# An mLSTM and two feed-forward layers: shorter state products, one integer pass, whole-tile stores

## The chip, the core and the metric

The kernel runs on one core of a Trainium2 chip. The time is device microseconds for one execution of the whole program, from inputs in HBM to outputs in HBM. A core has five engines with instruction queues of their own that meet through semaphores: TensorE (PE in the profile, PEld for the loads of its stationary operand), VectorE (DVE), ScalarE (ACT), GpSimd (POOL) and SyncE (SP), which here issues every DMA.

## What is computed

The reference is an mLSTM recurrence for two batches, 8 heads, 768 steps and head dimension 40, followed by two feed-forward layers on 1536 tokens of 320 features, each 320 to 2048 to 320:

```python
for t in range(S):
    m_new = maximum(f_gate[t] + m, i_gate[t])
    f_stab, i_stab = exp(f_gate[t] + m - m_new), exp(i_gate[t] - m_new)
    C = f_stab * C + i_stab * outer(v[t], k[t])
    n = f_stab * n + i_stab * k[t]
    y[t] = sigmoid(o_gate[t]) * (C @ q[t]) / maximum(abs(n @ q[t]), 1)
h = x @ w_in;  x = hinge(h) @ w_out        # hinge: h, 0 or (h + 1)**2 / 4
h = x @ w2_in; x = softplus(h) @ w2_out
```

## The kernel before

**The recurrence** is cut into 12 chunks of 64 steps (c = 0 to 11). The two batches lie in the two halves of the 128 partitions, so a chunk is a token tile of 128 rows. `attention(c, at)` (from line 393) does a chunk: loads of `qk` and `tok`, a scan on VectorE that makes the decay matrix, the products `qkp` (line 450) and `pv` (line 472), the product of the state with the decayed queries (line 480), which adds into `pv`, the new state's product `stp` (line 518), the decay of the state on GpSimd (line 522) and its addition on VectorE (line 528). Each of these products is 8 heads x 2 halves, one small matmul each. A head has 40 rows, but the halves are kept at 64 partitions: the product `stp` takes 64 columns of `tok` as stationary operand, and `state` has 64 rows in each half. A transpose (line 536) then brings the tile's result into the form that the first layer reads. The chunks with `n < EARLY` (4) are those of the first token block.

**The layers** work in three blocks of 512 tokens (j) and 16 slices of 128 hidden features (f): `up` (line 608, 8 matmuls) makes a slice of h, ScalarE and VectorE apply the hinge or softplus and split it into a high and a low part (`split_g`), and `down1` or `down2` (8 or 12 matmuls) adds the slice's part of the result, `LAG` = 3 steps behind `up`.

**The weights** come as 8-byte numbers, 704 of them per partition in one tile, 16 tiles for each layer. `weights(l, f)` (line 553) turns them into 4-byte floats: one load (line 558), two passes of ScalarE (lines 563 and 570: the upper word as a float scaled by 2^-112, and the top mantissa byte of the lower word, scaled to three bits), two integer passes of VectorE (line 574 shifts and joins, line 580 puts the sign in). `weights_split` (line 587) then makes the high part on ScalarE and the low part on VectorE or GpSimd. There are two `raw` buffers, so a load waits for the last pass that reads the tile two before.

**The tables of ScalarE** are loaded by the program where a phase begins (exp, sigmoid, softplus); where an instruction's function is not in the loaded table, the compiler puts one more load in front of it.

**The stores.** After the last slice of a block in `down2` the block's four token tiles are copied from PSUM, in turn by ScalarE and VectorE (lines 758 to 764), and each is stored by two DMAs on SP, one for each batch half (line 769).

**The order** of the instructions on every engine is written out ahead of time by the class `Plan` (line 34). Every task has an engine, a cost in us and a list of what it reads and writes; due times come from the positions (`at`) of TensorE's tasks, and each engine in turn takes the task that is ready and due first. A load's cost comes from `dma(kb)` (line 230), with `after` for its latency. TensorE gets filler matmuls (line 386) where nothing else is ready before the first `up`.

Of the kernel before, what the change touches and what calls it, by code (L numbers as in the profile page):

```python
# [8 lines left out]
F32R = mybir.dt.float32r  # L9
BF16 = mybir.dt.bfloat16  # L10
I32 = mybir.dt.int32
U8 = mybir.dt.uint8
ACTF = mybir.ActivationFunctionType
ALU = mybir.AluOpType
# [4 lines left out]
L = 128  # L19
# [158 lines left out]
def mlstm_moe_moe(ctx: ExitStack, tc: tile.TileContext, gates, qk, tok, ident, w1, w2, out):  # L178
# [36 lines left out]
    def vec(c):  # L215
        return 0.065 + c / 960
# [11 lines left out]
        return 0.1 + c / 430  # L228

    def dma(kb):  # L230
        return dict(cost=max(0.6, kb / 260), after=2.0)

    add = plan.add

# [155 lines left out]
    def attention(c, at):  # L390
# [5 lines left out]
        tk = lambda: tiles[TK]  # L396
        hd = lambda x: x.rearrange("p (h d) -> p h d", h=H)
        half = [slice(64 * i, 64 * i + 64) for i in range(2)]

        def t():  # L400
            nc.sync.dma_start(out=new("qk", QK, [128, 2, H, C]), in_=qk[c])
# [74 lines left out]
        if c > 0:  # L476
            def t():
                for h in range(H):
                    for p in half:
                        nc.tensor.matmul(  # L480
                            tiles["pv", n][p, h, :], tiles[QD][p, h, :], state[p, h, :], start=False, stop=(h == H - 1))
            add("pe", 1.0, t, duty=0.75, reads=[(QD,), (ST,)], writes=[(("pv", n),)], at=at[1] + 0.5)

        def t():
# [27 lines left out]
        if c < NC - 1:  # L512
            def t():
                ps = new("a", ("stp", n), [128, H, V1])
                for h in range(H):
                    k0 = H * V1 + DM + h * D
                    for p in half:
                        nc.tensor.matmul(ps[p, h, :], tk()[p, k0:k0 + 64], tiles[VE][p, h, :], start=True, stop=True)  # L518
            add("pe", 1.1, t, duty=0.75, reads=[(TK,), (VE,)], writes=[(("stp", n),)], new=[("a", ("stp", n))], at=at[1] + 1)
            if c > 0:  # L520
                def t():
                    nc.gpsimd.tensor_tensor(
                        out=state, in0=state, in1=tiles[DK][:, :, C - 1:C].to_broadcast([128, H, V1]), op=ALU.mult)
                add("pool", gps(328), t, port=True, reads=[(DK,)], writes=[(ST,)])

            def t():
                if c > 0:
                    nc.vector.tensor_tensor(out=state, in0=tiles["stp", n], in1=state, op=ALU.add)
                else:
                    nc.scalar.copy(state, tiles["stp", n])  # L530
            add("dve" if c > 0 else "act", vec(328), t, reads=[(("stp", n),)], writes=[(ST,)])

        def t():
            ps = new("a", ("tr", n), [128, 3, L])
# [15 lines left out]
        add("dve", vec(256) + vec(128) + 0.15, t, reads=[(("tr", n),)], writes=[(("xh", j), n), (("xl", j), n)])  # L550


    def weights(l, f):
        R, V, tag = ("raw", l, f), ("v", l, f), ("v", "v2")[l]

        def t():
            r = new("raw", R, [128, WC, 2], I32)
            nc.sync.dma_start(out=r, in_=(w1, w2)[l][f].bitcast(I32).rearrange("p (c w) -> p c w", w=2))
        add("sp", emit=t, writes=[(R,)], new=[("raw", R)], **dma(704))

        def t():
            v = new(tag, V, [128, WC], I32)
            nc.scalar.activation(
                out=v.bitcast(F32), in_=tiles[R][:, :, 1].bitcast(F32), func=ACTF.Copy, scale=2.0 ** -112)
        add("act", act(WC), t, reads=[(R,)] + ([*ATT] if l else []), writes=[(V,)], new=[(tag, V)])

        def t():
            r = tiles[R]
            top = r.rearrange("p c w -> p (c w)").bitcast(U8).rearrange("p (c w) -> p c w", w=8)[:, :, 3]
            nc.scalar.activation(out=r[:, :, 0], in_=top, func=ACTF.Copy, scale=1 / 32, bias=-31 / 64)  # L570
        add("act", act(WC), t, writes=[(R,)])

        def t():
            nc.vector.scalar_tensor_tensor(  # L574
                out=tiles[V], in0=tiles[V], scalar=3, in1=tiles[R][:, :, 0],
                op0=ALU.logical_shift_left, op1=ALU.bitwise_or)
        add("dve", vec(WC), t, port=True, reads=[(R,)], writes=[(V,)])

        def t():
            nc.vector.scalar_tensor_tensor(  # L580
                out=tiles[V], in0=tiles[R][:, :, 1], scalar=-0x80000000, in1=tiles[V],
                op0=ALU.bitwise_and, op1=ALU.bitwise_or)
        add("dve", vec(WC), t, port=True, reads=[(R,)], writes=[(V,)])

        weights_split(l, f, V)
# [146 lines left out]
    def down2(j, f, at):  # L732
# [21 lines left out]
        if e:  # L754
            for i in range(m):
                O = ("o", j, i)

                def t(i=i, O=O):
                    o = new("o", O, [128, DM])
                    if i % 2:  # L760
                        nc.vector.tensor_copy(o, tiles[dk[i]])
                    else:
                        nc.scalar.copy(o, tiles[dk[i]])
                add("dve" if i % 2 else "act", act(DM), t, reads=[*ATT, (dk[i],)], writes=[(O,)], new=[("o", O)])

                def t(i=i, O=O):
                    for b in range(B):
                        r0 = b * S + (t0 // L + i) * C
                        nc.sync.dma_start(out=out[r0:r0 + C, :], in_=tiles[O][64 * b:64 * b + 64, :])
                add("sp", emit=t, reads=[(O,)], **dma(160))  # L770

    softs = {}
    steps = [(l, j, f) for l in range(2) for j in range(len(BLOCKS)) for f in range(NF)]
# [103 lines left out]
```

## Time and profile before

| | |
|---|---|
| median of 3 runs | 442.21 us (441.85 to 443.28) |
| the profiled execution | 442.29 us |
| its span, first to last instruction | 440.5 us |
| mean granted clock of TensorE | 0.996 |
| busy: PE, PEld | 427.5 us (97%), 356.7 us (81%) |
| busy: DVE, ACT, POOL | 318.1 us (72%), 273.4 us (62%), 50.8 us (12%) |
| DMA | 41.11 MB, 12213 packets, 1904 of them under 512 B |

The profile is of one execution. Times in it count from the first instruction. A busy TensorE means that matmuls are in its pipeline. "Idle before" is the time that an engine waited in front of an instruction, with the engine or transfer that released it. In a stretch table "x" counts instructions, and the clock is the granted share of full speed.

### The profile page before, as it was taken

How to read it: one execution, taken by the hardware profiler on the slowest of the kernel's cores; microseconds unless marked ns; L12 is line 12 of the kernel's file. 1: busy time of each engine (PE TensorE's matmuls, PEld its weight loads, DVE VectorE, ACT ScalarE, POOL GpSimd, SP SyncE). 2: the span in 40 equal slices, each digit the busy share in tenths (PEclk: the TensorE clock that was granted, in tenths of full speed). 3: DMA queues.
4: the chain of work that ended last, by engine and by line, in shares of the span. 5: the costliest groups of instructions: out<-in, count | busy, mean ns of one | idle time of the engine just before them, and what ended most of it. 6: DMA issues, size and time to landing. Idle time of an engine off the chain costs nothing.

```text
span 440.5 us, 8190 instructions
## 1 busy us (share of the span) xinstructions
PE 427.5 (97%) x3319; PEld 356.7 (81%) x3319; DVE 318.1 (72%) x494; ACT 273.4 (62%) x473; POOL 50.8 (12%) x62
## 2 busy tenths in 40 slices
PE   8898899999999999999999999999999999999993
PEld 3676688877787878888888888999999999999993
DVE  6889999999968453567888889955565555655551
ACT  5525878767656354468999889655555555555551
POOL 2554112332221121000000000000000000000000
PEclk9999999999999999999999999999999999999998
DMA  5778766447440300014234441000020000110002
GB/s 210 222 255 258 252 208 205 168 149 251 139 179 3 116 1 1 1 49 150 91 119 176 141 132 65 2 0 0 1 58 4 0 1 0 31 31 1 0 1 60
DMA packets 12213, 41.11 MB, mean 93 GB/s; under 512 B 1904, under 2 KB 3568, under 8 KB 12176
## 3 DMA queue, kind: packets, MB, share of 16 engines
q1 hardware_dynamic: 12176, 40.59, 28.2%
q8 instruction: 26, 0.43, 0.4%
q14 instruction: 11, 0.09, 0.1%
HBM read 38.57 MB, written 2.02 MB: 92 GB/s over the span
## 4 chain that ended last, share of the span: by engine, by line
PE 76%; DVE 12%; ACT 6%; DMA 3%; issue 1%; SPq 1%; ACTq 0%
PE h L619 32%; PE d L691 3%; PE d L690 3%; PE d L692 3%; PE d L749 3%; PE a L751 3%; PE a L750 3%; PE a L749 3%; PE d L751 3%; PE d L750 3%; PE qkp L450 2%; DVE v L574 2%; PE pv L472 2%; PE d L686 2%; PE stp L518 2%; PE pv L480 2%
## 5 line engine op out<-in xcount | busy, mean ns | idle before, releaser
L619 PE MATMUL h<-xh,w 128*128 128x512 f32 x576 | 178.3, 392 | 1.9 <-DVE u L636 1.3
L619 PEld LDWEIGHTS h<-xh,w 128*128 128x128 f32 x576 | 108.0, 188 | 25.1 <-DVE u L636 1.8
L672 DVE TENSOR_TENSOR gl<-u,gh 128x512 fp32r<-128x512 f32 x96 | 66.7, 696 | 35.8 <-ACT gh L668 32.2
L668 ACT CAST gh<-u 128x512 fp32r<-128x512 f32 x96 | 59.3, 619 | 48.3 <-DVE u L659 31.4
L619 PE MATMUL h<-xl,w 128*128 128x512 f32 x192 | 75.4, 393 | 1.0 <-DVE xl L546 1.0
L659 DVE TENSOR_TENSOR u<-u,e 128x512 f32<-128x512 f32 x48 | 33.1, 692 | 29.1 <-ACT e L655 29.1
L655 ACT ACTIVATE e<-e 128x512 f32<-128x512 f32 x48 | 30.3, 632 | 32.3 <-DVE e L650 32.3
L636 DVE SCALAR_TENSOR_TENSOR u<-u,h 128x512 f32<-128x512 f32 x48 | 32.7, 682 | 15.5 <-ACT u L632 15.3
L619 PEld LDWEIGHTS h<-xl,w 128*128 128x128 f32 x192 | 36.1, 188 | 6.9 <-DVE xl L546 1.3
L627 ACT ACTIVATE u<-h 128x512 f32<-128x512 f32 x48 | 28.5, 593 | 20.3 <-PE h L619 20.0
L691 PE MATMUL d<-gh,w 128*128 128x512 f32 x96 | 37.5, 391 | 0.0
L690 PE MATMUL d<-gh,w 128*128 128x512 f32 x96 | 37.5, 391 | 0.0
L692 PE MATMUL d<-gl,w 128*128 128x512 f32 x96 | 37.4, 389 | 0.0
L574 DVE SCALAR_TENSOR_TENSOR v<-v,raw 128x704 int32<-128x704 int32 x32 | 29.6, 924 | 9.5 <-ACT raw L570 9.2
L650 DVE SCALAR_TENSOR_TENSOR e<-u,h 128x512 f32<-128x512 f32 x48 | 32.9, 685 | 4.9
L646 ACT ACTIVATE u<-h 128x512 f32<-128x512 f32 x48 | 28.6, 596 | 8.8 <-PE h L619 8.7
L599 DVE TENSOR_TENSOR w<-v,w 128x64 fp32r<-128x64 f32 (+2 forms) x48 | 31.1, 675 | 1.5 <-ACT w L592 1.4
L632 ACT ACTIVATE u<-u 128x512 f32<-128x512 f32 x48 | 30.3, 631 | 0.7
L749 PE MATMUL d<-w,gh 128*128 128x320 f32 x96 | 29.7, 309 | 0.5 <-DVE xl L717 0.5
L751 PE MATMUL a<-w,gl 128*128 128x320 f32 x96 | 29.7, 309 | 0.0
L751 PE MATMUL d<-w,gl 128*128 128x320 f32 x96 | 29.7, 309 | 0.0
L750 PE MATMUL a<-w,gh 128*128 128x320 f32 x96 | 29.6, 309 | 0.0
(92 smaller groups left out, 701.3 us busy)
## 6 DMA issues: line engine op xcount, KB each, us to landing
raw<-in_w_dram SPq DMA_DIRECT2D x32, 704.0 KB, 4.1
qk<-in_qk_dram SPq DMA_DIRECT2D x12, 512.0 KB, 4.8
tok<-in_tok_dram SPq DMA_DIRECT2D x12, 496.0 KB, 4.3
dec<-scr_d SPq DMA_DIRECT2D x22, 128.0 KB, 4.0
out_dram<-o SPq DMA_DIRECT2D x24, 80.0 KB, 2.1
consts<-in_ident_dram SPq DMA_DIRECT2D x1, 132.0 KB, 2.2
gf<-in_gates_dram SPq DMA_DIRECT2D x1, 48.0 KB, 1.9
gi<-in_gates_dram SPq DMA_DIRECT2D x1, 48.0 KB, 1.9
```

Source lines behind the costliest of these rows:

```text
L574: nc.vector.scalar_tensor_tensor(out=tiles[V], in0=tiles[V], scalar=3, in1=tiles[R][:, :, 0], op0=ALU.logical_shift_left, op1=ALU.bitwise_or)
L619: nc.tensor.matmul(hp, a, x, start=(i == 0), stop=(i == len(ops) - 1))
L650: nc.vector.scalar_tensor_tensor(out=new("e", E, [128, n]), in0=tiles[M], scalar=-2.0, in1=tiles[HP], op0=ALU.mult, op1=ALU.add)
L659: nc.vector.tensor_tensor(out=tiles[M], in0=tiles[M], in1=tiles[E], op=ALU.add)
L668: nc.scalar.copy(new("gh", GH, [128, n], F32R), tiles[G])
L672: nc.vector.tensor_tensor(out=new("gl", GL, [128, n], F32R), in0=tiles[G], in1=tiles[GH].bitcast(F32), op=ALU.subtract)
L690: nc.tensor.matmul(d[i], hi[:, k], gh, start=s, stop=False)
L691: nc.tensor.matmul(d[i], lo[:, k], gh, start=False, stop=False)
L692: nc.tensor.matmul(d[i], hi[:, k], gl, start=False, stop=e)
L749: nc.tensor.matmul(d, gh[:, k], hi, start=s, stop=False)
L750: nc.tensor.matmul(d, gh[:, k], lo, start=False, stop=False)
L751: nc.tensor.matmul(d, gl[:, k], hi, start=False, stop=e)
```

## The change

It touches five places. The state product reads 40 of the 64 rows of each half, in all chunks after the first, and for chunks from 4 on `stp` takes 40 columns as stationary operand, writes 40 rows in each half, and the state is added in two instructions of 40 partitions; the planner gives that product 0.75 us instead of 1.1. The weights' load writes its bytes one place further in the tile. ScalarE's two passes become two Prelu instructions: the first turns the top byte, read as a signed integer, into a value in V, the second turns V, in place, into the integer of sign and upper exponent bits; VectorE then shifts the word that begins at the fourth byte by five and joins it, in one pass. A token tile is stored by one DMA from 128 partitions, with a target of three dimensions (batch, row, feature), and the last tile is copied in two halves by ScalarE and VectorE. The planner reckons loads with 330 GB/s and at least 0.45 us, instead of 260 GB/s and 0.6.

```diff
--- before.py
+++ after.py
@@ -9,6 +9,7 @@
 F32R = mybir.dt.float32r
 BF16 = mybir.dt.bfloat16
 I32 = mybir.dt.int32
+I8 = mybir.dt.int8
 U8 = mybir.dt.uint8
 ACTF = mybir.ActivationFunctionType
 ALU = mybir.AluOpType
@@ -228,7 +229,7 @@
         return 0.1 + c / 430
 
     def dma(kb):
-        return dict(cost=max(0.6, kb / 260), after=2.0)
+        return dict(cost=max(0.45, kb / 330), after=2.0)
 
     add = plan.add
 
@@ -396,6 +397,7 @@
         tk = lambda: tiles[TK]
         hd = lambda x: x.rearrange("p (h d) -> p h d", h=H)
         half = [slice(64 * i, 64 * i + 64) for i in range(2)]
+        keys = [slice(64 * i, 64 * i + D) for i in range(2)]
 
         def t():
             nc.sync.dma_start(out=new("qk", QK, [128, 2, H, C]), in_=qk[c])
@@ -476,9 +478,9 @@
         if c > 0:
             def t():
                 for h in range(H):
-                    for p in half:
+                    for p, k in zip(half, keys):
                         nc.tensor.matmul(
-                            tiles["pv", n][p, h, :], tiles[QD][p, h, :], state[p, h, :], start=False, stop=(h == H - 1))
+                            tiles["pv", n][p, h, :], tiles[QD][k, h, :], state[k, h, :], start=False, stop=(h == H - 1))
             add("pe", 1.0, t, duty=0.75, reads=[(QD,), (ST,)], writes=[(("pv", n),)], at=at[1] + 0.5)
 
         def t():
@@ -514,9 +516,10 @@
                 ps = new("a", ("stp", n), [128, H, V1])
                 for h in range(H):
                     k0 = H * V1 + DM + h * D
-                    for p in half:
-                        nc.tensor.matmul(ps[p, h, :], tk()[p, k0:k0 + 64], tiles[VE][p, h, :], start=True, stop=True)
-            add("pe", 1.1, t, duty=0.75, reads=[(TK,), (VE,)], writes=[(("stp", n),)], new=[("a", ("stp", n))], at=at[1] + 1)
+                    for p, k in zip(half, keys):
+                        o, w = (p, 64) if n < EARLY else (k, D)
+                        nc.tensor.matmul(ps[o, h, :], tk()[p, k0:k0 + w], tiles[VE][p, h, :], start=True, stop=True)
+            add("pe", 1.1 if n < EARLY else 0.75, t, duty=0.75, reads=[(TK,), (VE,)], writes=[(("stp", n),)], new=[("a", ("stp", n))], at=at[1] + 1)
             if c > 0:
                 def t():
                     nc.gpsimd.tensor_tensor(
@@ -524,11 +527,12 @@
                 add("pool", gps(328), t, port=True, reads=[(DK,)], writes=[(ST,)])
 
             def t():
-                if c > 0:
-                    nc.vector.tensor_tensor(out=state, in0=tiles["stp", n], in1=state, op=ALU.add)
+                if c == 0:
+                    nc.scalar.copy(state, tiles["stp", n])
                 else:
-                    nc.scalar.copy(state, tiles["stp", n])
-            add("dve" if c > 0 else "act", vec(328), t, reads=[(("stp", n),)], writes=[(ST,)])
+                    for r in [slice(0, 128)] if n < EARLY else keys:
+                        nc.vector.tensor_tensor(out=state[r], in0=tiles["stp", n][r], in1=state[r], op=ALU.add)
+            add("dve" if c > 0 else "act", vec(328) * (1 if n < EARLY else 2), t, reads=[(("stp", n),)], writes=[(ST,)])
 
         def t():
             ps = new("a", ("tr", n), [128, 3, L])
@@ -550,36 +554,33 @@
         add("dve", vec(256) + vec(128) + 0.15, t, reads=[(("tr", n),)], writes=[(("xh", j), n), (("xl", j), n)])
     def weights(l, f):
         R, V, tag = ("raw", l, f), ("v", l, f), ("v", "v2")[l]
 
         def t():
-            r = new("raw", R, [128, WC, 2], I32)
-            nc.sync.dma_start(out=r, in_=(w1, w2)[l][f].bitcast(I32).rearrange("p (c w) -> p c w", w=2))
+            r = new("raw", R, [128, 2 * WC + 2], I32)
+            nc.sync.dma_start(out=r.bitcast(U8)[:, 1:8 * WC + 1], in_=(w1, w2)[l][f].bitcast(U8))
         add("sp", emit=t, writes=[(R,)], new=[("raw", R)], **dma(704))
 
         def t():
             v = new(tag, V, [128, WC], I32)
+            top = tiles[R].bitcast(I8).rearrange("p (c w) -> p c w", w=8)[:, 1:WC + 1, 0]
+            nc.scalar.activation(out=v.bitcast(F32), in_=top, func=ACTF.Prelu, bias=-56.0, alpha=2.0 ** -40)
+        add("act", act(WC), t, reads=[(R,)] + ([*ATT] if l else []), writes=[(V,)], new=[(tag, V)])
+
+        def t():
             nc.scalar.activation(
-                out=v.bitcast(F32), in_=tiles[R][:, :, 1].bitcast(F32), func=ACTF.Copy, scale=2.0 ** -112)
-        add("act", act(WC), t, reads=[(R,)] + ([*ATT] if l else []), writes=[(V,)], new=[(tag, V)])
-
-        def t():
-            r = tiles[R]
-            top = r.rearrange("p c w -> p (c w)").bitcast(U8).rearrange("p (c w) -> p c w", w=8)[:, :, 3]
-            nc.scalar.activation(out=r[:, :, 0], in_=top, func=ACTF.Copy, scale=1 / 32, bias=-31 / 64)
-        add("act", act(WC), t, writes=[(R,)])
-
-        def t():
+                out=tiles[V], in_=tiles[V].bitcast(F32), func=ACTF.Prelu, scale=2.0 ** 27, bias=112 * 2.0 ** -13,
+                alpha=2.0 ** 40)
+        add("act", act(WC), t, writes=[(V,)])
+
+        def t():
+            mid = tiles[R].rearrange("p (c w) -> p c w", w=2)[:, 0:WC, 1]
             nc.vector.scalar_tensor_tensor(
-                out=tiles[V], in0=tiles[V], scalar=3, in1=tiles[R][:, :, 0],
-                op0=ALU.logical_shift_left, op1=ALU.bitwise_or)
-        add("dve", vec(WC), t, port=True, reads=[(R,)], writes=[(V,)])
-
-        def t():
-            nc.vector.scalar_tensor_tensor(
-                out=tiles[V], in0=tiles[R][:, :, 1], scalar=-0x80000000, in1=tiles[V],
-                op0=ALU.bitwise_and, op1=ALU.bitwise_or)
+                out=tiles[V], in0=mid, scalar=5, in1=tiles[V], op0=ALU.logical_shift_right, op1=ALU.bitwise_or)
         add("dve", vec(WC), t, port=True, reads=[(R,)], writes=[(V,)])
 
         weights_split(l, f, V)
@@ -755,19 +756,27 @@
             for i in range(m):
                 O = ("o", j, i)
 
+                def copies(parts, j=j, i=i, O=O):
+                    for e, c0, c1 in parts:
+                        def t(e=e, c0=c0, c1=c1):
+                            o = tiles[O] if O in tiles else new("o", O, [128, DM])
+                            o, d = o[:, c0:c1], tiles[dk[i]][:, c0:c1]
+                            if e == "dve":
+                                nc.vector.tensor_copy(o, d)
+                            else:
+                                nc.scalar.copy(o, d)
+                        add(e, act(c1 - c0), t, reads=[*ATT, (dk[i],)], writes=[(O, c0)],
+                            new=[("o", O)] if c0 == 0 else [])
+
+                if j == len(BLOCKS) - 1 and i == m - 1:
+                    copies([("act", 0, DM // 2), ("dve", DM // 2, DM)])
+                else:
+                    copies([("dve" if i % 2 else "act", 0, DM)])
+
                 def t(i=i, O=O):
-                    o = new("o", O, [128, DM])
-                    if i % 2:
-                        nc.vector.tensor_copy(o, tiles[dk[i]])
-                    else:
-                        nc.scalar.copy(o, tiles[dk[i]])
-                add("dve" if i % 2 else "act", act(DM), t, reads=[*ATT, (dk[i],)], writes=[(O,)], new=[("o", O)])
-
-                def t(i=i, O=O):
-                    for b in range(B):
-                        r0 = b * S + (t0 // L + i) * C
-                        nc.sync.dma_start(out=out[r0:r0 + C, :], in_=tiles[O][64 * b:64 * b + 64, :])
-                add("sp", emit=t, reads=[(O,)], **dma(160))
+                    r0 = (t0 // L + i) * C
+                    nc.sync.dma_start(out=out.rearrange("(b s) d -> b s d", b=B)[:, r0:r0 + C, :], in_=tiles[O])
+                add("sp", emit=t, reads=[(O, 0), (O, DM // 2)], **dma(160))
 
     softs = {}
     steps = [(l, j, f) for l in range(2) for j in range(len(BLOCKS)) for f in range(NF)]
```

## Rows read from the trace of the kernel before

**Rows 1.** Busy time by stretch: PE, PEld, DVE, ACT, POOL, clock, DMA share, GB/s.
```profile
10.00:41.40 31.40, 30.04 (x549) 21.18 (x547) 27.87 (x46) 13.52 (x32) 15.76 (x20) 1.00 0.74 240
41.40:60.00 18.60, 16.08 (x176) 12.29 (x177) 18.47 (x29) 15.56 (x27) 4.77 (x7) 1.00 0.78 240
60.00:121.00 61.00, 60.57 (x617) 48.65 (x616) 58.08 (x98) 44.50 (x78) 16.77 (x16) 1.00 0.56 185
...
260.00:278.00 18.00, 17.52 (x90) 15.08 (x89) 16.39 (x25) 16.80 (x29) 0.00 (x0) 1.00 0.24 81
```

**Rows 2.** Timeline of PE at the first `up`: start, us, instruction.
```profile
41.38 0.51 PE L619 MATMUL h<-xh,w 128*128 128x512 f32 x1
```

**Rows 3.** Timeline of the last 8 us.
```profile
432.92 4.94 SPq L769 DMA_DIRECT2D out_dram<-o  x8
...
433.79 0.49 DVE L761 COPY o<-a 128x320 f32<-128x320 f32 x1 [0.39 <-PE a L751]
```

**Rows 4.** Chain of waits: start, us, what.
```profile
38.41 6.59 DMA tok<-in_tok_dram
...
140.92 1.08 PE qkp L450 x32
...
147.87 0.93 PE stp L518 x32
...
281.14 1.84 PE h L619 x8
284.74 1.84 PE h L619 x8
```

**Rows 5.** Groups by form: busy us, mean ns | idle before, releaser.
```profile
L632 ACT ACTIVATE u<-u 128x512 f32<-128x512 f32 x48 | 30.3, 631 | 0.7
...
L580 DVE SCALAR_TENSOR_TENSOR v<-raw,v 128x704 int32<-128x704 int32 x32 | 29.4, 918 | 0.1
...
L570 ACT ACTIVATE raw<-raw 128x704 int32<-128x704 uint8 x32 | 27.0, 844 | 0.0
L592 ACT CAST w<-v 128x704 fp32r<-128x704 f32 x32 | 24.8, 777 | 6.6 <-DVE v L580 5.8 <-PE d L692 0.4
...
L528 DVE TENSOR_TENSOR state<-stp,state 128x328 f32<-128x328 f32 x10 | 4.7, 466 | 0.1
```

**Rows 6.** Stretch before the first `up`, L574 alone: us, DVE busy (x instructions).
```profile
10.00:41.40 31.40, 1.76 (x2) 1.00 0.74 240
```

**Rows 7.** DMA issues on the page: KB each, median us to landing.
```profile
raw<-in_w_dram SPq DMA_DIRECT2D x32, 704.0 KB, 4.1
...
tok<-in_tok_dram SPq DMA_DIRECT2D x12, 496.0 KB, 4.3
...
out_dram<-o SPq DMA_DIRECT2D x24, 80.0 KB, 2.1
```

**Rows 8.** Waits of SP's queue: us in total, times, longest.
```profile
SPq L558 <- DVE v L580: 154.0, 27, 44.8
```

**Rows 9.** Timeline of ACT: table loads and weight passes.
```profile
154.54 1.28 ACT L799 ACT_TABLE_LOAD   x1
...
168.35 1.28 ACT L489 ACT_TABLE_LOAD   x1
...
258.97 1.28 ACT L655 ACT_TABLE_LOAD   x1 [1.34 <-DVE e L650]
...
262.67 0.85 ACT L563 ACTIVATE v<-raw 128x704 f32<-128x704 f32 x1
...
273.96 0.87 ACT L570 ACTIVATE raw<-raw 128x704 int32<-128x704 uint8 x1
```

**Rows 10.** DMA of the last 8.5 us: packets, MB, share.
```profile
DMA packets 640, 0.66 MB, mean 77 GB/s; under 512 B 128, under 2 KB 640, under 8 KB 640
...
q1 hardware_dynamic: 640, 0.66, 31.7%
```

**Rows 11.** Busy time by stretch, 12 to 14 us.
```profile
12.00:14.00 2.00, 2.00 (x11) 0.98 (x12) 1.91 (x4) 1.93 (x8) 2.00 (x3) 1.00 1.02 364
```

More of the change, by code (lines that the diff above doesn't have):

```diff
@@ L562, in t @@
             v = new(tag, V, [128, WC], I32)
-            nc.scalar.activation(
-                out=v.bitcast(F32), in_=tiles[R][:, :, 1].bitcast(F32), func=ACTF.Copy, scale=2.0 ** -112)
+            top = tiles[R].bitcast(I8).rearrange("p (c w) -> p c w", w=8)[:, 1:WC + 1, 0]
+            nc.scalar.activation(out=v.bitcast(F32), in_=top, func=ACTF.Prelu, bias=-56.0, alpha=2.0 ** -40)
         add("act", act(WC), t, reads=[(R,)] + ([*ATT] if l else []), writes=[(V,)], new=[(tag, V)])
         def t():
-            r = tiles[R]
-            top = r.rearrange("p c w -> p (c w)").bitcast(U8).rearrange("p (c w) -> p c w", w=8)[:, :, 3]
-            nc.scalar.activation(out=r[:, :, 0], in_=top, func=ACTF.Copy, scale=1 / 32, bias=-31 / 64)
-        add("act", act(WC), t, writes=[(R,)])
+            nc.scalar.activation(
+                out=tiles[V], in_=tiles[V].bitcast(F32), func=ACTF.Prelu, scale=2.0 ** 27, bias=112 * 2.0 ** -13,
+                alpha=2.0 ** 40)
+        add("act", act(WC), t, writes=[(V,)])
         def t():
+            mid = tiles[R].rearrange("p (c w) -> p c w", w=2)[:, 0:WC, 1]
             nc.vector.scalar_tensor_tensor(
-                out=tiles[V], in0=tiles[V], scalar=3, in1=tiles[R][:, :, 0],
-                op0=ALU.logical_shift_left, op1=ALU.bitwise_or)
-        add("dve", vec(WC), t, port=True, reads=[(R,)], writes=[(V,)])
-        def t():
-            nc.vector.scalar_tensor_tensor(
-                out=tiles[V], in0=tiles[R][:, :, 1], scalar=-0x80000000, in1=tiles[V],
-                op0=ALU.bitwise_and, op1=ALU.bitwise_or)
+                out=tiles[V], in0=mid, scalar=5, in1=tiles[V], op0=ALU.logical_shift_right, op1=ALU.bitwise_or)
         add("dve", vec(WC), t, port=True, reads=[(R,)], writes=[(V,)])
```

## The prediction

> **What bounds the kernel now.** I read the page's busy times first (TensorE leads), then a table of stretches, the chain of waits, the costliest groups by form, and last the two ends. The stretches show where TensorE isn't busy. In 60 to 121 us it has 0.43 us of idle time and in 260 to 278, the busiest later stretch of ScalarE and VectorE, 0.48, all at granted clock 1.00, the 2.4 GHz level [rows 1]. So behind 60 us only shorter TensorE work moves the end. Ahead of it VectorE is the full engine: 18.47 of 18.6 us in 41.4 to 60, where TensorE idles 2.5 us, and 27.87 of 31.4 us in 10 to 41.4, where the first `up` starts [rows 1, 2]. The end is a tail: the last copy starts at 433.79, and eight stores that SP issues one after another from 432.92 fill the time to 440.5 [rows 3]. The profiled execution took 442.29, 1.8 us more than its span and 0.1 over the median of 442.21; I sum against 442.29.
>
> **Part 1, 40 stationary columns (c = 4 to 10, seven `stp` tasks).** All seven stand behind 60 us, on the bound. The chain of waits gives one `stp` 0.93 us for 32 records, and `qkp`, with the same 64 stationary columns but 64 moving ones instead of 41, 1.08 [rows 4]. No row has 40 stationary columns. At least nothing is saved; in proportion to the columns it is 0.93 x 24/64 = 0.35 us. The nearest rows say that 23 columns on the other operand are worth 0.15 us. I take 0.2: 7 x 0.2 = **-1.4 us** (0 to -2.4). The state product over 40 instead of 64 rows keeps its moving and stationary columns: 0. VectorE's add becomes two of 40 partitions; it has as many elements per partition, so 7 x 0.47 = 3.3 us are added [rows 5]. They are hidden by what part 2 takes from VectorE; without that they would land in stretches with 3 us free in 61.
>
> **Part 2, one integer pass.** It removes one of two passes of 0.92 us for each of 32 weight tiles, 29.4 us of VectorE [rows 5]. ScalarE keeps two: the byte pass stays like L570 (844 ns, the same stride), the second reads 704 contiguous words as the cast of L592 does (777), so ScalarE gets 32 x 0.07 = 2.1 us back, hidden. The second now reads what the first wrote; the hinge has such an in-place pair on the same engine, and it idled 0.7 us in 48 [rows 5]: 0. What is the VectorE time worth? Two tiles' passes stand before 41.4 us [rows 6]. There the gain is at most two passes, 1.8 us; from there to 60 at most the idle 2.5 us: 4.3 together. What is late next there is TensorE's own order and the loads. Behind 60 us it buys at most the 0.9 us of idle time.
>
> The load lands one byte off. No row has such a target. At best it costs nothing, at worst the moving part of the 4.1 us (all above the 2.1 of a small store [rows 7]) doubles, 2 us a tile. I take 0, as the loads' issue mostly waited for VectorE: 154 us in 27 waits of SP for L580, the last pass of a tile [rows 8].
>
> **Part 3, loads at 330 GB/s in the planner.** This changes no work, only order, on SP and behind it on every engine. A `tok` load issued at 38.41, behind two weight loads, took 6.59 us instead of 4.3 [rows 4, 7]. If the new order puts weight loads ahead of two more such loads on the chain, 2 x 2.3 = 4.6 us are lost. With part 2's gain the early stretch is worth between +4.6 and -4.3; I take **-2**, since every weight load also waits for one pass less.
>
> **Part 4, ScalarE's tables.** The trace shows three loads in order: the table for softplus loaded at 154.54, `Abs` made a load of 1.28 us necessary at 168.35, and Softplus another at 258.97 [rows 9]. So the softplus table does not hold every function, and the new Prelu may be one that it lacks. After the first Softplus ScalarE still has weight passes, in five groups between Softplus instructions, the first at 262.67 and the last at 273.96 [rows 9]. If Prelu is missing, each costs a load there and one back: 10 x 1.28 = 12.8 us on an engine that is busy 16.80 of 18 us there [rows 1]. If not, nothing. ScalarE's idle time (1.2) and about one step of 3.6 us [rows 4] absorb some of it, since `down2` runs three steps behind `up` and two `h` buffers stand between: 12.8 - 1.2 - 3.6 = 8. With a pass less the weight tiles come through sooner, so I count two groups, 5.1 us, and of these nearly all absorbed: **+1** (0 to +11.6).
> The Trainium skill, "ScalarE: Activation LUTs", section "Table sets: the hidden batching unit", says that the cheap functions (relu, copy, identity, abs) are filler in every set. The load for `Abs` at 168.35 says otherwise; by the page's sentence this term would rather be 0.
>
> **Part 5, one store for a token tile.** Before, 8 stores of 64 rows left 640 packets in the last 8.5 us: 512 of 1280 bytes and 128 under 512 bytes, 16 for each store, one for each engine [rows 10]. The new store has on the DRAM side an outermost extent of 2 (the batch halves), then 64 rows. No row has a transfer whose outermost extent is under 16, so both ends are open.
> Spread over 16 engines: four issues instead of eight. At 4.94 / 8 = 0.62 us each [rows 3] from 432.92 the last starts at 434.8, after the halved copy; landing takes 2.1 us [rows 7] and four more packets per engine 0.34: it ends at 437.2, **-3.3 us**.
> Dealt by the outermost extent: two engines carry four stores, 256 packets each. A store's packet costs 31.7% x 16 x 8.5 us / 512 = 84 ns when 16 engines write at once; the fastest loads, 364 GB/s at share 1.02, come to 22.3 GB/s for an engine or 57 ns for 1280 bytes [rows 10, 11]. Two engines alone are nearer to the second; I take 60 ns: 15.4 us, and 2.1 - 0.34 = 1.76 for issue and completion, 17.2 us from the first issue where there were 7.6: **+9.6** (8.9 to 15.7). The earlier blocks' stores have some 58 us each and nothing behind them: hidden.
> I take the second as the likelier, since rows of 64 and 16 have always been dealt whole to 16 engines and a deal by the outermost dimension is the plainest that does this, while nothing shows one that looks further in.
> The Trainium skill, "DMA: Bandwidth & Descriptors", section "Rules for kernel authors", states it so: an outermost dimension of c < 16 confines the whole transfer to at most c engines. The trace agrees only as far as its 16 small packets per store go. By its section on two partition halves (one transfer of 128 partitions is better than two) part 5 would instead gain, as in the first reading.
>
> **Sum.** 442.29 - 1.4 - 2 + 1 + 9.6 = **449.5 us**.
>
> **The rivals.**
> Spread stores (the other side: faster): the tail gives 3.3 us back instead. For it: all stores so far ran on 16 engines, and SP's eight issues of 0.62 do set the tail. Against: the outer extent of 2. It decides between four and eight engines: 128 packets x 60 ns and 1.76 are 9.4 us, over today's 7.6, 64 packets are 5.6. 442.29 - 1.4 - 2 + 1 - 3.3 = 436.6.
> Tables or late loads eat it: the stores are spread, but Prelu switches tables in all five groups (+8 instead of +1: 443.6) or the loads go the wrong way (+4.6 instead of -2: 443.2). For it: the `Abs` load, the 6.59 us. Against: weights that finish before 259 need no switch.
> The change doesn't do what it says: 40 columns run no faster; 1.4 us more in either case (450.9 or 438.0).
>
> **How the numbers follow.** Two engines 0.62; spread 0.30; spread with the gain eaten 0.08, about 443.4. The two-engine case alone lies in 446 to 457 (its tail from +8.9 to +15.7, the early stretch and the tables each way). For eight in ten the range must reach into the spread case: 435 to 455. A difference under 0.3% (1.3 us) can't be told from none here. Faster: 0.30 and a quarter of 0.08, 0.32. Same: 0.04, from the third case and the lucky end of the first. Slower: 0.64.
>
> **What would show it.** Part 1: `stp` from c = 4 on at 0.7 to 0.75 us instead of 0.93. Part 2: 32 integer passes and VectorE some 26 us less busy; the first `up` before 41.4. Part 4: table loads beyond five, behind 259. Part 5: 2 small packets for a store instead of 16 and a tail of about 17 us after the first of the last four issues; 16 small packets and an end 3 us after the last copy would prove me wrong, and the time would be near 436. A first `up` after 42 would say that the order of loads cost more than the pass gave.

## The result, and the profile after

The changed kernel takes 449.13 us (median of 4 runs, 448.74 to 450.19) where the kernel before takes 442.08 in the same comparison: a ratio of 1.015 (95% interval 1.0127 to 1.0174), slower by 7 us. The forecast was 449.5. Medians and ratios here and below leave out executions that were disturbed as a whole; of two experiments the profiled execution was such a one, and no trace of them is used.

The profiled execution took 448.74 us, with a span of 447.0. The page: busy time by engine, granted clock in 40 slices (the last two, 8 and 5, hold the tail, in which TensorE has nothing more to do), packets.
```profile
PE 426.2 (95%) x3315; PEld 353.6 (79%) x3315; DVE 292.7 (65%) x467; ACT 273.0 (61%) x474; POOL 52.7 (12%) x64
...
PEclk9999999999999999999999999999999999999985
...
DMA packets 11853, 41.11 MB, mean 92 GB/s; under 512 B 1544, under 2 KB 3208, under 8 KB 11816
```
VectorE is 25.4 us less busy (318.1 before). The packets under 512 bytes fell by 360: 12 stores with 2 each in place of 24 with 16.

Busy time by stretch, columns as in [rows 1]:
```profile
10.00:41.40 31.40, 30.80 (x558) 21.40 (x554) 26.43 (x49) 16.50 (x36) 16.96 (x19) 1.00 0.88 288
41.40:60.00 18.60, 17.39 (x183) 13.23 (x184) 17.04 (x30) 16.06 (x29) 6.58 (x7) 1.00 0.60 196
60.00:121.00 61.00, 61.00 (x598) 49.29 (x597) 50.43 (x87) 44.05 (x78) 15.74 (x19) 1.00 0.57 192
```
Behind 60 us TensorE no longer waits, and VectorE has 7.7 us less to do in 60 to 121. But the first `up` comes at 42.25 us, 0.87 later than in [rows 2], and it waits for ScalarE's copy of the transposed tokens. One trace doesn't fix this number: in six traces whose kernels have the same instructions on TensorE in the same order (this one and five of the variants below) the first `up` comes at 41.1 to 42.7 us. The timeline of PE:
```profile
42.25 0.49 PE L620 MATMUL h<-xh,w 128*128 128x512 f32 x1 [1.17 <-ACT xh L545]
```
From the first `up` to the start of the last matmul (less 0.04 us), first before, then after: length, busy time of PE and PEld, and so on.
```profile
41.38:433.40 392.02, 388.59 (x2718) 331.81 (x2719) 283.10 (x435) 254.43 (x430) 31.88 (x35) 1.00 0.24 78
```
```profile
42.25:430.80 388.55, 388.19 (x2718) 329.20 (x2719) 258.40 (x405) 249.93 (x424) 31.86 (x37) 1.00 0.22 74
```
The middle is shorter by 3.47 us, and nearly all of it is idle time: 3.43 before, 0.36 after. TensorE's busy time fell by only 0.40, though the state products became shorter. Groups of instructions by form, and one `stp` in the chain of waits:
```profile
L521 PE MATMUL stp<-ve,tok 64*40 64x41 f32 x224 | 5.5, 198 | 0.0
...
L582 DVE SCALAR_TENSOR_TENSOR v<-raw,v 128x704 int32<-128x704 int32 x32 | 28.4, 891 | 10.4 <-ACT v L575 10.4
```
```profile
65.38 0.61 PE stp L521 x32
```
0.61 us instead of the 0.93 of [rows 4], seven times, is 2.3 us. As much is lost again in the `up` products, which run at 394 to 395 ns. The group of line 619 before, and of line 620 after:
```profile
L619 PE MATMUL h<-xh,w 128*128 128x512 f32 x576 | 178.3, 392 | 1.9 <-DVE u L636 1.3 <-DVE w L599 0.4
L619 PE MATMUL h<-xl,w 128*128 128x512 f32 x192 | 75.4, 393 | 1.0 <-DVE xl L546 1.0
```
```profile
L620 PE MATMUL h<-xh,w 128*128 128x512 f32 x576 | 180.5, 395 | 1.2 <-ACT xh L545 1.2
L620 PE MATMUL h<-xl,w 128*128 128x512 f32 x192 | 75.7, 394 | 0.0
```
That is 2.5 us more in the same 768 products; the other 0.6 us by which TensorE's busy time fell are not assigned. Last the tail, which answers to [rows 3]. The last matmul before, then the timeline after, and the DMA of 430.2 to 447 us after:
```profile
433.44 0.31 PE L751 MATMUL a<-w,gl 128*128 128x320 f32 x1
```
```profile
430.32 6.09 SPq L778 DMA_DIRECT2D out_dram<-o  x4
...
430.84 0.31 PE L752 MATMUL a<-w,gl 128*128 128x320 f32 x1
```
```profile
GB/s 0 0 0 24 40 34 30 18 37 49 49 49 49 49 49 55 49 49 49 49 49 49 49 49 52 52 49 49 49 49 49 49 49 49 55 49 43 0 0 0
DMA packets 520, 0.66 MB, mean 39 GB/s; under 512 B 8, under 2 KB 520, under 8 KB 520
...
q1 hardware_dynamic: 520, 0.66, 11.2%
```
From the start of the last matmul to the end it takes 447.0 - 430.84 = 16.2 us, where it took 440.5 - 433.44 = 7.1. Four stores leave 8 small packets, 2 each, and the same 0.66 MB flows at 49 GB/s, where [rows 10] had a mean of 77 with idle time in it. SP's four issues take longer than the eight before (6.09 us against 4.94), but they end at 430.32 + 6.09 = 436.4, and the data flow on at 49 GB/s for another 9 us. So the rate sets this tail, not the issuing. In sum: +0.87 (first `up`) - 3.07 (idle time) - 0.40 (TensorE's work) + 9.10 (tail) = +6.5 us, the difference of the two spans.

### The profile page after: what moved, and what is told of

Read it like the earlier page. It is cut to its first block, busy times and chain, and to the rows that moved or that the text cites. A ratio compares the mean times of both kernels' runs of the same rounds, so it can differ in the third digit from the quotient of the medians.

```text
span 447.0 us, 8134 instructions
## 1 busy us (share of the span) xinstructions
PE 426.2 (95%) x3315; PEld 353.6 (79%) x3315; DVE 292.7 (65%) x467; ACT 273.0 (61%) x474; POOL 52.7 (12%) x64
## 4 chain that ended last, share of the span: by engine, by line
PE 87%; DMA 4%; DVE 3%; ACT 1%; issue 1%; SPq 0%; POOL 0%; ACTq 0%; DVEq 0%
PE h L620 38%; PE d L692 5%; PE d L691 5%; PE d L693 5%; PE d L751 3%; PE a L751 3%; PE a L752 3%; PE d L752 3%; PE d L750 3%; PE a L750 3%; PE d L687 3%; PE d L688 2%; PE qkp L452 2%; PE pv L474 2%; DMA raw<-in_w_dram 2%; PE pv L482 1%
## 5 line engine op out<-in xcount | busy, mean ns | idle before, releaser
L620 PE MATMUL h<-xh,w 128*128 128x512 f32 x576 | 180.5, 395 | 1.2 <-ACT xh L545 1.2
L620 PEld LDWEIGHTS h<-xh,w 128*128 128x128 f32 x576 | 108.0, 188 | 25.4 <-ACT xh L545 1.4
L673 DVE TENSOR_TENSOR gl<-u,gh 128x512 fp32r<-128x512 f32 x96 | 67.7, 706 | 41.1 <-ACT gh L669 37.0
L582 DVE SCALAR_TENSOR_TENSOR v<-raw,v 128x704 int32<-128x704 int32 x32 | 28.4, 891 | 10.4 <-ACT v L575 10.4
L571 ACT ACTIVATE v<-raw 128x704 f32<-128x704 int8 x32 | 27.0, 844 | 8.1 <-DMA raw<-in_w_dram 4.8
L600 DVE TENSOR_TENSOR w<-v,w 128x704 fp32r<-128x704 f32 (+2 forms) x46 | 29.4, 666 | 3.7 <-ACT w L593 3.5
```

Of the source, the lines that this page charges most:

```text
L620: nc.tensor.matmul(hp, a, x, start=(i == 0), stop=(i == len(ops) - 1))
L673: nc.vector.tensor_tensor(out=new("gl", GL, [128, n], F32R), in0=tiles[G], in1=tiles[GH].bitcast(F32), op=ALU.subtract)
```

## The experiments

My theory: the stores cost 9 us and hide a gain of some 2 us, made of the shorter state products and the emptied early stretch, less a slower pace of the `up` products. Rivals for each stand with the expectations. "Two stores" is the changed kernel with the stores of before, the base for most of what follows.

### Part 5, the stores

**Two stores.** The changed kernel with
```diff
-nc.sync.dma_start(out=out.rearrange("(b s) d -> b s d", b=B)[:, r0:r0 + C, :], in_=tiles[O])
+for b in range(B):
+    r0 = b * S + (t0 // L + i) * C
+    nc.sync.dma_start(out=out[r0:r0 + C, :], in_=tiles[O][64 * b:64 * b + 64, :])
```


> The changed kernel with the stores of before: two DMAs of 64 rows for each token tile, everything else and the order of every engine as in the changed kernel. Theory (the one store is dealt to two engines): the last matmul starts where it does in the changed kernel (430.8 us), the last four tiles leave 128 small packets instead of 8, and the end comes 7 us after the last matmul as before instead of 16: span 437.9, about 439.7 us. Rival (the tail is long because SP's issue of a store became longer, or because the halved last copy comes later): the tail stays over 12 us and the time over 445.

Measured 440.09 us, 0.9948 of before (0.9919 to 0.9978). The tail is back at 437.3 - 430.34 = 7.0 us, and it has 128 small packets again. Timeline of the last matmul, and the DMA of 429 to 437.4 us:
```profile
430.34 0.31 PE L752 MATMUL a<-w,gl 128*128 128x320 f32 x1
```
```profile
DMA packets 640, 0.66 MB, mean 78 GB/s; under 512 B 128, under 2 KB 640, under 8 KB 640
```

**The kernel before with one store**: the same edit the other way round in the kernel before, nothing else.

> The kernel before with nothing changed but the store: one DMA of 128 partitions for each token tile. Theory: 8 small packets in the tail, about 50 GB/s over it, 16.7 us from the first of the last four issues to the end instead of 7.6: 442.1 + 9.1 = 451.2 us. Rival (one store is as good as two and the loss came from another part): 439 to 442.

Measured 451.06 us, 1.0197 (1.018 to 1.0215): +8.8. The two together show part 5 as cause, with and without the other parts: 449.13 - 440.09 = 9.0 there, 8.8 here. Its DMA from 432 to 449 us is the changed kernel's, 520 packets with 8 under 512 bytes.

**Two stores in the last block alone**, the single store kept in the first two blocks.
```diff
+if j < len(BLOCKS) - 1:
     nc.sync.dma_start(out=out.rearrange("(b s) d -> b s d", b=B)[:, r0:r0 + C, :], in_=tiles[O])
+else:
+    for b in range(B):
+        nc.sync.dma_start(out=out[b * S + r0:b * S + r0 + C, :], in_=tiles[O][64 * b:64 * b + 64, :])
```


> The changed kernel with one store for a tile in the first two token blocks and two stores in the last. Theory (the earlier blocks' slow stores have 58 us each and nothing behind them): the same as with two stores everywhere, 439.7 us, within 0.3%. Rival (a transfer that runs 14 us on two engines holds up something, a buffer of the copies or the fetching of instructions): slower than that by more than 0.3%.

Measured 441.55 us, 0.9977 (0.995 to 1.0004). The median is 1.5 us, or 0.33%, above that of two stores, just past the mark of the rival, but the intervals overlap, and no cost of the earlier blocks' stores is shown. The profiled execution has the short tail (442.3 - 435.32 = 7.0 us). It is 5 us longer than the one of two stores ahead of that, but not where the stores are: the first is issued at 325.9 us, and from 300 to 420 us both kernels get through the same 667 matmul records. The time is lost in the early stretch, where TensorE's granted clock fell to the 1.2 GHz level for a while. The stretch table of this kernel (PE, PEld, DVE, ACT, POOL, clock, DMA share, GB/s):
```profile
40.00:42.00 2.00, 1.16 (x5) 0.54 (x5) 2.00 (x4) 1.08 (x3) 1.53 (x1) 1.00 1.04 319
42.00:44.00 2.00, 1.63 (x5) 1.23 (x5) 1.69 (x5) 0.54 (x1) 1.44 (x2) 0.73 0.72 218
44.00:46.00 2.00, 2.00 (x6) 1.54 (x6) 1.40 (x2) 1.50 (x3) 0.00 (x0) 0.50 0.26 46
```
The fall stands behind 1.21 us of idle time in 40 to 44 us. The executions scatter with it: of ten of two stores, the six with a mean clock of 0.995 or 0.996 lie at 438.6 to 440.1 us, the two with 0.988 at 442.7 and 444.3. What decides whether the clock falls is open: the changed kernel's trace has 1.21 us of idle time in the same 4 us and kept 1.00.

**Two queues.** Two stores, those of the second batch in the last block issued by ScalarE.
```diff
-nc.sync.dma_start(out=out[r0:r0 + C, :], in_=tiles[O][64 * b:64 * b + 64, :])
+q = nc.scalar if b and j == len(BLOCKS) - 1 else nc.sync
+q.dma_start(out=out[r0:r0 + C, :], in_=tiles[O][64 * b:64 * b + 64, :])
```


> The changed kernel with two stores for a tile, and in the last block the second batch half issued by ScalarE's queue instead of SP's. Theory (what is left of the tail is SP issuing eight stores of 0.62 us one after another): the last store is issued some 2.3 us earlier, span 435.6, 437.4 us. Rival (the landing of the data sets the end, or ScalarE's copies are held up by its own issues): no better than with one queue, 439.7.

Measured 437.74 us, 0.9882 (0.9842 to 0.9922), as expected; of its four executions two took 436.0 and 436.3 us and two 439.2. The timeline of its last 6 us:
```profile
431.83 2.66 SPq L780 DMA_DIRECT2D out_dram<-o  x4
432.32 0.59 ACTq L780 DMA_DIRECT2D out_dram<-o  x1
...
432.35 0.31 PE L752 MATMUL a<-w,gl 128*128 128x320 f32 x1
...
433.06 1.78 ACTq L780 DMA_DIRECT2D out_dram<-o  x3
```
Eight issues take 3.0 us side by side instead of 4.94 in a row, and the tail is 437.4 - 432.35 = 5.1 us where it was 7.0. So before the change it was the issuing, not the engines' rate, that set the tail; the change halved the issues and lost the engines.

### Parts 1 to 3, the middle

**Part 1 undone** (on two stores): 64 columns and one addition again, with their costs in the planner; the state is still read over 40 rows.
```diff
-o, w = (p, 64) if n < EARLY else (k, D)
+o, w = p, 64
```


> The changed kernel with the two 64-row stores of before, and with part 1 undone: all state products of the seven later blocks take 64 stationary columns again, at their old cost in the planner. Compared with the kernel that has only the two stores given back (440.09 us). Theory: a block's chain of 32 state products costs 0.93 us of TensorE with 64 columns and 0.61 us with 40, so seven blocks give 7 x 0.32 = 2.3 us back: 442.4 us, with the product's mean near 228 ns where it was 198, and TensorE busy all the same. Rival: the 32 records only overlap differently and the engine is not held longer: 440.1 us, and the steps of the state stage are as long as with 40 columns.

Measured 441.39 us, 0.9977 (0.9948 to 1.0005): 1.3 us more than two stores, between the two numbers, and the intervals overlap. Not decided by itself.

**Part 1 alone**, in the kernel before, with its planner costs.

> The kernel before with part 1 alone: 40 stationary columns for the state products of the seven later blocks, contraction over 40 rows where the state is read, and the two additions of 40 partitions instead of one of 128. Weight passes, planner costs, addresses and stores are those of before. Theory: 32 records take 0.61 us instead of 0.93, 7 x 0.32 = 2.3 us less TensorE time on the path that sets the end: 440.0 us, with VectorE about 7 x 0.48 = 3.4 us busier and no new wait. Rival: the gain is eaten by VectorE, which sets the pace of the early stretch and now has a second addition of 0.48 us in each of the later blocks: 441.5 to 442.5 us, with idle time of TensorE ahead of up products grown by as much as the products save.

Measured 441.77 us, 0.9992 (0.9974 to 1.0011). The 2.3 us (a ratio of 0.9948) lie outside; the rival's number was right. The products did become shorter:
```profile
L520 PE MATMUL stp<-ve,tok 64*40 64x41 f32 x224 | 5.6, 200 | 0.0
```
but the profiled execution lost the gain in the early stretch, where its clock fell twice (stretches of 4 us, columns as above):
```profile
18.00:22.00 4.00, 4.00 (x78) 3.71 (x75) 1.46 (x4) 1.35 (x4) 0.72 (x1) 0.61 0.29 90
46.00:50.00 4.00, 4.00 (x29) 3.02 (x28) 4.00 (x7) 2.27 (x4) 1.03 (x1) 0.70 0.50 162
```
The rival's mechanism, more idle time ahead of `up` products, is not shown by that: 2.1 us before `up` here and 2.7 in the kernel before. What is shown is that part 1 alone moves the time by less than it takes from TensorE. Part of that is the clock: the five executions with a mean clock of 0.995 or more have a median of 441.28 us, the fourteen such of the kernel before 442.03, which is 0.75 us. Where the rest of the 2.3 goes stays open.

**Part 2 undone** (on two stores): the four passes and the raw tile of before.
```diff
-nc.scalar.activation(out=v.bitcast(F32), in_=top, func=ACTF.Prelu, bias=-56.0, alpha=2.0 ** -40)
+nc.scalar.activation(out=v.bitcast(F32), in_=tiles[R][:, :, 1].bitcast(F32), func=ACTF.Copy, scale=2.0 ** -112)
...
+nc.vector.scalar_tensor_tensor(
+    out=tiles[V], in0=tiles[V], scalar=3, in1=tiles[R][:, :, 0],
+    op0=ALU.logical_shift_left, op1=ALU.bitwise_or)
...
```


> The changed kernel with the two 64-row stores of before and with part 2 undone: the weights are unpacked by the passes of before (VectorE builds the low word in a pass of its own), and the raw tile has its old size, so the weight tiles stand at the addresses of before. Two things are expected by the theory that part 2 emptied the early stretch and that the weight tile's address sets the pace of the up products: VectorE is busy some 25 us longer and TensorE waits again between 41.4 and 60 us, about 2 us more than the 0.45 us of the kernel with two stores, while the mean of the up products goes from 394 back to 389 ns (-2.5 us): 439 to 441 us, and the two parts can be read apart in the trace. Rival 1: the early stretch was emptied by part 3 (the order) alone: no wait comes back and the time is 437.6 us. Rival 2: the up products' pace has nothing to do with the address: they stay at 394 ns, and the time is 442 to 443 us.

Measured 448.82 us, 1.0104 (1.0056 to 1.0152): 8.7 us more than two stores by the medians, 6.9 by the ratios, and above all three expectations. The first `up` comes at 45.15, and TensorE waits for VectorE and ScalarE ahead of it and behind: in 60 to 121 us, where the kernel with two stores has no idle time, it idles 5.45 us. Timeline, stretch and longest waits of PE (us in total, times, longest):
```profile
45.15 0.51 PE L626 MATMUL h<-xh,w 128*128 128x512 f32 x1
```
```profile
60.00:121.00 61.00, 55.55 (x537) 42.80 (x537) 58.18 (x93) 43.17 (x75) 14.20 (x14) 1.00 0.59 190
```
```profile
PE qkp L452 <- DVE y L505: 2.0, 1, 2.0
PE tr L540 <- ACT y L511: 1.9, 1, 1.9
```
One part of the expectation held: the `up` products are back at 392 and 393 ns. The kernel with part 1 alone has the same passes and the same products, but the order of the old planner costs (and the last copy in one piece), and takes 441.77 us. So most of the loss comes with the order that the planner makes of the old passes with the costs of parts 1 and 3, and what part 2 is worth depends on it. Which of those costs does it (part 3's is the likelier) was not separated.

**Part 3 undone** (on two stores).
```diff
-return dict(cost=max(0.45, kb / 330), after=2.0)
+return dict(cost=max(0.6, kb / 260), after=2.0)
```


> The changed kernel with the two 64-row stores of before, and with part 3 undone: the order is made with 260 GB/s and a floor of 0.6 us for a load, as before. Theory: the early stretch was emptied by the fewer VectorE passes, and part 3 only moved the loads forward, which put the DMA queues at a share of 0.9 instead of 0.75 between 10 and 41.4 us and the first up product at 41.6 to 42.3 us instead of 41.4: the time stays within 1.5 us of 440.1, the first up product comes at or before 41.4 us. Rival: part 3 carries the gain of the early stretch: TensorE idles again by 2 us or more between 41.4 and 60 us, and the time is 442 us or more.

Measured 439.33 us, 0.9928 (0.9904 to 0.9951), within the 1.5 us of the theory. Part 3 doesn't carry the gain. The expected place of the first `up` can't be read here; a later kernel with this order shows it. Eight of eleven executions lie within 439.1 to 439.6 us, where those of two stores scatter over 5.6.

### The pace of the `up` products

From 300 to 420 us the kernels have the same instructions on the same tiles, but a product takes a different time in them. The raw tile of the changed kernel has 8 bytes more in each partition, 5640; two of them, rounded up to 5664 each, put all tiles behind them, the weights among these, 64 bytes further on.

**Raw tile longer** (on two stores): the weights stand 128 bytes behind their place in the kernel before; the order is the same.
```diff
-r = new("raw", R, [128, 2 * WC + 2], I32)
+r = new("raw", R, [128, 2 * WC + 16], I32)
```


> The changed kernel with the two 64-row stores of before, and one number more: the raw tile has 2*WC + 16 words a partition where the changed kernel has 2*WC + 2. Every instruction and its place in the order is the same; only the addresses of the tiles behind it (the weight tiles among them) move by 64 bytes, to the same place within 128 bytes that they had in the kernel before. Theory: the up products run at 394 ns instead of 389 in the changed kernel because the 8 bytes put on each raw tile moved the weight tiles by 64 bytes: the mean comes back to 389 ns, 768 x 0.003 to 0.005 = 2.3 to 3.8 us go, and the time is 436.5 to 438 us. Rival: the pace comes from something else (other traffic in SBUF, the layout of the low halves): 394 ns and 440.1 us stay.

Measured 442.66 us, 0.9964 (0.9929 to 0.9999). Its executions scatter from 437.8 to 444.0, so that the median lies above that of before (442.33) and the ratio under 1; no gain against two stores is shown. The mean of the products stays at 395 ns: the form of the theory that looks at 128 bytes fell.

**Tiles moved by 1 KiB** (on two stores): the weights stand 1024 bytes behind their old place.
```diff
+const.tile([128, 240], F32, name="gap")
```


> The changed kernel with the two 64-row stores of before and an unused tile of 960 bytes a partition between the token tiles and the raw tiles: nothing else differs, the instructions and their order are the same. The weight tiles then stand 1024 bytes behind their place in the kernel before (they stand 64 bytes behind it in the changed kernel, and 128 bytes in the one with the longer raw tile). Theory: the pace of the up products depends on the weight tiles' address within some power of two up to 1024 bytes, as three sets of addresses gave three sets of times in the layer-1 stage, where the kernels have the same instructions: the products of xh return to 389 ns and those of xl to 393 to 395 ns there, all of them to 389 ns between 62 and 190 us, and the time is 437 to 438 us. Rival: what counts is larger than 1 KiB, or is not the address: the means stay at 392 to 395 ns and the time is 440 to 441 us.

The pace came back to what it was. The products of the `up` line in 300 to 420 us (ns: shortest/median/longest, first and last start), in turn: before, after (+64 bytes), raw tile longer (+128), tiles moved (+1024).
```profile
L619 PE MATMUL h<-xh,w x202: 389/389/395, 299.6 to 419.1; 128*128 128x512 f32 x101
```
```profile
L620 PE MATMUL h<-xh,w x202: 392/393/398, 299.9 to 419.9; 128*128 128x512 f32 x101
```
```profile
L620 PE MATMUL h<-xh,w x201: 390/392/404, 299.8 to 419.7; 128*128 128x512 f32 x101
```
```profile
L621 PE MATMUL h<-xh,w x201: 389/389/395, 300.5 to 419.8; 128*128 128x512 f32 x101
```
The other traces agree, whatever else their kernels change: these products have the same shortest, median and longest (389/389/395) in the three other traces with the old addresses and in the other one with 1024 bytes, and 392/393/398 in the four others with 64 bytes. So the addresses set the pace. What in them does (a tile's place against that of the other operand, or against other engines' accesses) stays open. The time, 439.52 us or 0.9931 (0.9897 to 0.9965), missed the 437 to 438 expected: the scatter of 436.8 to 442.0 covers the 2.5 us, and the time alone doesn't show them.

### Together, and the price of a table

**Parts 1 and 2, two queues, the order with 260 GB/s, and the gap**: the three edits shown above on two stores.

> What the runs so far speak for, in one kernel: parts 1 and 2 of the change; the order made with 260 GB/s; two 64-row stores a token tile, in the last block from two queues; the unused 960 bytes that bring the weight tiles to their old place within 1024 bytes. From 439.3 us (order with 260 GB/s): -2.7 us if the two queues bring what they brought (437.7 against 440.1, 437.4 expected), and -2.5 us if the address theory is right: 434.5 to 436 us. If the address theory is wrong: 436.5 to 437.5 us. It also gives the trace of the early stretch with the order of 260 GB/s: by the theory that part 2 alone emptied it, the first up product comes at or before 41.4 us and TensorE idles less than 1 us between 41.4 and 60 us.

Measured 433.9 us (433.74 to 435.48), 0.9825 (0.9809 to 0.9841): 8.2 us faster than the kernel before, the fastest of all, a bit below what was expected with the address theory, and further below the 436.5 to 437.5 without it. Its `up` products are at 391 and 393 ns. First `up` and early stretch:
```profile
41.49 0.50 PE L621 MATMUL h<-xh,w 128*128 128x512 f32 x1 [0.57 <-ACT xh L546]
```
```profile
41.40:60.00 18.60, 17.55 (x184) 13.48 (x185) 16.81 (x31) 16.20 (x30) 5.56 (x7) 1.00 0.84 277
```
The marks set for part 2 alone (41.4, and under 1 us idle) are missed by 0.1 us or less.

**Three v2 buffers** (on two stores): the last weights are unpacked after the first Softplus.
```diff
-                den=2, y=2, v2=10, e=3, o=4, h=2, d0=1, d1=1, d2=1, a=3)
+                den=2, y=2, v2=3, e=3, o=4, h=2, d0=1, d1=1, d2=1, a=3)
```


> The changed kernel with the two 64-row stores of before, and 3 buffers instead of 10 for the unpacked layer-1 weights, so that the last weights are unpacked after the first Softplus: the Prelu passes of two weight tiles then stand between hinges of layer 1, and ScalarE reloads its tables 12 times instead of 5. It prices the term that the prediction put at +1 us (0 to +11.6) and that the changed kernel didn't have to pay. Theory: the 7 reloads of 1.28 us take 9.0 us of ScalarE in the stretch from 255 to 290 us, where the changed kernel has ScalarE busy for some 12 us of 18; the hinges wait for two reloads in a row (2.6 us) at each change, which the two h buffers, a product of 3.6 us each, mostly cover: TensorE idles there by 1 to 4 us and the time is 441 to 444 us. Rival 1: the reloads hold the chain up in full: 449 us. Rival 2: they cost nothing: 440 us, and TensorE is busy all the time between 255 and 290 us.

Measured 447.82 us, 1.0119 (1.0079 to 1.0158): 7.7 us more than two stores, nearer to the 449 of the first rival than to the theory. There are 13 table loads, eight more and not seven: each of the four Prelu passes needs one and the Softplus behind it another. TensorE idles 4.85 us in 255 to 290 us, where 1 to 4 were expected. ScalarE's timeline between two Softplus steps, and two of the stretches:
```profile
263.23 1.28 ACT L656 ACT_TABLE_LOAD   x1
...
265.17 1.28 ACT L575 ACT_TABLE_LOAD   x1
266.46 0.79 ACT L575 ACTIVATE v<-v 128x704 int32<-128x704 f32 x1
```
```profile
265.00:270.00 5.00, 2.53 (x10) 1.76 (x9) 3.41 (x5) 4.95 (x7) 0.00 (x0) 0.96 0.00 0
270.00:275.00 5.00, 4.50 (x18) 3.25 (x17) 3.85 (x7) 4.91 (x9) 0.00 (x0) 0.70 0.00 0
```
The idle time of 2.47 us in 265 to 270 is followed by a granted clock of 0.70.

## Why the prediction was right, step by step

The time came out within 0.4 us, and that closeness is in part luck. Of the sum's four terms two were right in size; the errors of the other two, and of one that was missing, cancelled. What decided the direction, the store dealt to fewer engines, was right in its mechanism.

- **Part 5, +9.6: right, +9.1 in the trace and 8.8 to 9.0 by experiment.** 2 small packets a store, and 11.2% x 16 x 16.8 us / 512 = 59 ns for a packet, where 60 was taken. From the first issue to the end it took 16.7 us (17.2). No view counts the engines: two is read from the 2 small packets, where a store on 16 engines left 16, and from the rate. The rule that the Trainium skill gives in "DMA: Bandwidth & Descriptors", section "Rules for kernel authors", that an outermost extent under 16 confines the transfer to as many engines, agrees with 2 small packets a store and 49 GB/s. The row on two partition halves in the same section of the Trainium skill, by which one transfer should be no worse than two, does not hold for a target whose outermost extent is 2: here it lost 8.8 to 9.1 us, and the measurement decides.
- **Parts 2 and 3, -2: right in the sum, wrong in the place.** -2.2 us (+0.87 at the first `up`, -3.07 of idle time). I had the first `up` before 41.4, and said that one after 42 would mean that the order cost more than the pass gave. It came at 42.25 (41.1 to 42.7 in the six traces with this order on TensorE), and the step that failed is that inference: the start moved back here, and the waits behind it went all the same. That part 3 adds to the gain was not borne out either (439.3 without it).
- **Part 1, -1.4: mis-sized.** The records went from 0.93 to 0.61 us, -2.3, close to the proportion of the columns (-2.4), not to the nearest rows. I said that VectorE's additions are hidden only by part 2. Part 1 alone indeed brought 0.3 us of the 2.3, but that the additions are the reason isn't shown.
- **Part 4, +1: 0 here.** Five loads, as before: the last Prelu stands just ahead of the first Softplus.
```profile
254.83 0.78 ACT L575 ACTIVATE v<-v 128x704 int32<-128x704 f32 x1
255.74 1.28 ACT L656 ACT_TABLE_LOAD   x1
```
  The two groups that I counted don't exist, as the weight passes end sooner. The mechanism is real: two tiles behind the first Softplus made eight loads more and cost 7.7 us. So the term is 0, but not for what I read in the Trainium skill, "ScalarE: Activation LUTs", section "Table sets: the hidden batching unit": its list of functions in every set doesn't name Prelu, and these loads show that the softplus table lacks it.
- **What no step had: +2.5 us** for the `up` products, from 8 bytes more in a tile that they never read. I called the byte offset of the load free and did not ask what the longer tile moves.

## What to carry to other kernels

Fewer DMAs are a gain only where the one that replaces them is dealt to as many engines: count the small packets per transfer (16 or 2) before and after, and if issuing is the bound, use a second queue. A tile that grows by a few bytes moves its neighbours, and a matmul's pace can change with it by 1%: compare the mean of an untouched group first. A saving on one engine need not show in the time: 2.3 us less of TensorE alone brought 0.3. And a planner's costs that serve one set of passes can make an order that costs 7 to 9 us with another.

## What was not expected of the hardware

- 768 products of 128 x 512 took 253.7 us, 256.2 with all tiles behind `raw` 64 bytes further on, and 253.3 with them 1024 bytes further on.
- A fall of TensorE's granted clock from 1.00 to 0.50 for some 2 to 6 us, behind idle time of 1 to 2.5 us, came in some traces, at 18, 30, 43, 46, 105 or 270 us, and not in others whose kernels have the same order on TensorE. Much of the scatter of the variants goes with it.
- Stationary columns count nearly in proportion: 24 of 64 fewer took 0.32 of 0.93 us from 32 small products.
